# Moving GpSimd folds off a chunk's last slot, and packing the last transform stage one item to a slot

## The chip, the cores and the metric

One core of one Trainium2 chip. The metric is the device time of one execution in microseconds (us), the median of several executions. Engines are written as in the profile: PE is TensorE (matmuls), PEld its weight loads, ACT is ScalarE, DVE is VectorE, POOL is GpSimd, SP is SyncE, which here issues most DMAs. A "q" after an engine (SPq, ACTq) marks what its sequencer does, such as issuing a DMA.

## The reference, cut to what matters

```python
X = np.fft.fft(x, axis=1); X = np.fft.fft(X, axis=2)   # x: 8 x 3008 x 256, float32
x = X.real.reshape(24064, 256)
out = (gelu(x @ w_gate) * (x @ w_val)) @ w_out         # 256 -> 1536 -> 256
```

A real two-axis Fourier transform of each of 8 batches, then a gated feed-forward layer on every token.

## The kernel before

The order of the program is planned by hand. A batch's feed-forward work takes 36 slots: three chunks of columns (512, 512 and 481) by 12 blocks of the hidden dimension. Into these slots the plan puts the transform of the next batch: folds on POOL, stage 1 on PE, a trip through memory (Z), and nine last-stage items, three for each chunk: a row item (`tp_y`), an even item (`tp_e`) and an odd item (`tp_o`). I name a stretch of 36 slots after the batch that is *transformed* in it: stretch 3 transforms batch 3 while PE multiplies for batch 2.

```python
def tp_y(b, gi):                      # the row item: 4 x 128 numbers, copied by ACT, written to memory
    ...
    nc.scalar.activation(yr[:, :], ps[:4, 0:128], AF.Copy)
    nc.sync.dma_start(out=<yrow in memory, part gi>, in_=yr[:, :])

def tp_rows(b, gi):                   # one slot after the odd item of chunk gi
    nc.sync.dma_start(out=<EB, part gi, all 128 partitions>, in_=<yrow, part gi>)
    nc.sync.dma_start(out=<EO, odd half, part gi, 1 partition>, in_=<yrow, part gi>)   # "the odd row"

def plan():
    ...
    slot_of = [first + i * n // len(ops) for i in range(len(ops))]      # folds of batch b
    if b == 1: slot_of = [4, 4, 5, 5, ...]
    for s, f in zip(slot_of, ops): at(pool, s, f)
    if 1 < b < B - 1:                                                   # input loads for batch b + 1
        for k, piece in ((0, 1), (1, 3), (2, 4)):
            at(fill, slot_of[piece * per + 1] + 1, lambda b=b, k=k: load_part(b + 1, k))
    ...
    items = [tp_y(b, 0), tp_e(b, 0), tp_o(b, 0), tp_y(b, 1), ...]       # nine
    spread(b, items, s + 7, s0 + NS - 3)                                # from slot s + 7 to the stretch's slot 33
```

`load_part` with k = 0 is a pair of loads of 768 KB: the forward part by SP, the mirrored part by POOL. The writes to EO are tracked by tile: an odd item, which writes EO too, waits for the odd row's DMA of the chunk before it.

## Time and profile before

| | before |
|---|---|
| median of 3 executions | 630.39 us (629.39 to 630.58) |
| span of the profiled execution | 627.0 us |
| mean granted clock of PE | 0.996 |
| length of stretches 1 to 7, and of the last without transform | 78.17, 75.69, 74.04, 73.92, 73.92, 73.93, 72.91, 81.13 us |

The stretches are measured from the start of a first gate matmul to that of the next. Four of them last about 74 us, which is what PE's work takes. The prediction shows the busy times, the chain of waits and the waits.

It did not make the row quick: POOL's half of the pair had left at 224.96, the row took 4.7 us (by the semaphore updates it landed at 230.51, where such rows take 1.8 to 2.4 us in this trace with no load under way), and ACT waited half a microsecond for it:

```profile
230.59 0.60 ACT L592 ACTIVATE EO_sb<-ps_dft 128x512 bf16<-128x512 f32 x1 [0.51 <-DMA EO_sb<-yrow]
```

### The profile page before, as it was taken

The numbers are of one execution on the slowest core, as the hardware profiler recorded it, in microseconds if no ns is written. First come the engines' busy times: TensorE is split into PE (matmuls) and PEld (weight loads), VectorE is DVE, ScalarE is ACT, GpSimd is POOL, SyncE is SP. The second block draws the span as 40 slices with busy tenths as digits, with TensorE's granted clock in tenths as the row PEclk, the third lists the DMA queues.
The fourth block names the chain that finished last, engine by engine and source line by source line (L and its number), as shares of the span: only waits on it lengthen the run. The fifth ranks groups of instructions, "written<-read, shape, count | busy, mean of one in ns | idle before, by whom it ended". The sixth has DMA issues, their size and how long they took to land.

```text
span 627.0 us, 12895 instructions
## 1 busy us (share of the span) xinstructions
PE 612.3 (98%) x4195; PEld 405.1 (65%) x4243; DVE 578.3 (92%) x941; ACT 428.4 (68%) x842; POOL 505.3 (81%) x510
## 2 busy tenths in 40 slices
PE   7999999999999999999999999999999999999997
PEld 3456666666666666666666666666666666666666
DVE  8689989999899999999999998999999999999992
ACT  6777677666776677667676677676676666666661
POOL 8399999989897998879997899969988655555651
PEclk8999999999999999999999999999999999999999
DMA  9961754536353353731645335633212322221123
GB/s 177 227 97 31 210 129 116 144 105 159 99 146 101 98 133 79 184 113 46 160 110 135 101 78 127 148 97 98 62 49 63 91 86 55 51 52 39 42 51 81
DMA packets 54217, 65.40 MB, mean 104 GB/s; under 512 B 7831, under 2 KB 49802, under 8 KB 51754
## 3 DMA queue, kind: packets, MB, share of 16 engines
q1 hardware_dynamic: 47222, 49.03, 30.6%
q0 software_dynamic: 6608, 15.29, 11.4%
q8 instruction: 33, 0.54, 0.4%
q10 hardware_dynamic: 320, 0.26, 0.2%
q14 instruction: 34, 0.28, 0.2%
HBM read 39.65 MB, written 30.17 MB: 111 GB/s over the span
## 4 chain that ended last, share of the span: by engine, by line
PE 93%; ACT 2%; issue 1%; DVE 1%; DMA 1%; POOL 1%; POOLq 0%; ACTq 0%
PE ps_o L749 38%; PE ps_g L660 28%; PE ps_v L660 19%; PE ps_dft L546 2%; PE ps_dft L582 2%; PE ps_o L820 1%; DMA Z_sb<-z 1%; PE ps_dft L443 1%; PE ps_dft L612 0%; ACT gelu_sb L676 0%; POOL h_sb L724 0%; POOL eo_sb L224 0%; DMA out_dram<-out_sb 0%; ACT gelu_sb L685 0%; PE ps_dft L749 0%
## 5 line engine op out<-in xcount | busy, mean ns | idle before, releaser
L724 POOL TENSOR_TENSOR h_sb<-gelu_sb,v_sb 128x512 bf16<-128x512 bf16 (+1 forms) x280 | 319.8, 1146 | 93.1 <-DVE v_sb L722 85.9
L749 PE MATMUL ps_o<-Wo_sb,h_sb 128*128 128x256 bf16 (+1 forms) x2232 | 334.9, 273 | 0.9 <-POOL h_sb L724 0.9
L749 PEld LDWEIGHTS <-h_sb 128*128 128x128 bf16 (+1 forms) x2304 | 228.7, 100 | 112.9 <-POOL h_sb L724 2.6
L676 ACT ACTIVATE gelu_sb<-ps_g 128x512 bf16<-128x512 f32 (+1 forms) x288 | 169.4, 588 | 98.6 <-PE ps_g L660 80.9
L660 PE MATMUL ps_g<-EO_sb,W_sb 128*128 128x512 bf16 (+1 forms) x817 | 228.5, 375 | 3.8 <-ACT gelu_sb L685 0.8
L704 DVE SCALAR_TENSOR_TENSOR ve_sb<-EB_sb,yw,ps_v 128x512 f32<-128x512 bf16 (+1 forms) x280 | 206.3, 737 | 25.9 <-PE ps_v L660 25.0
L660 PE MATMUL ps_v<-EO_sb,W_sb 128*128 128x512 bf16 (+1 forms) x575 | 213.7, 375 | 0.7 <-DVE W_sb L451 0.6
L720 DVE TENSOR_TENSOR h_sb<-gelu_sb,ps_v 128x512 bf16<-128x512 bf16 (+1 forms) x280 | 189.9, 678 | 1.1 <-ACT gelu_sb L685 0.7
L660 PEld LDWEIGHTS <-W_sb 128*128 128x128 bf16 x1440 | 137.2, 98 | 81.1 <-issue 1.8
L722 DVE SCALAR_TENSOR_TENSOR v_sb<-ve_sb,ps_v 128x512 f32<-128x512 f32 (+1 forms) x280 | 187.5, 670 | 0.0
L685 ACT ACTIVATE gelu_sb<-ps_g 128x512 bf16<-128x512 f32 (+1 forms) x288 | 168.7, 586 | 0.0
L769 ACT ACTIVATE out_sb<-ps_o 128x512 f32<-128x512 f32 x92 | 55.0, 598 | 35.7 <-PE ps_o L749 35.6
L224 POOL TENSOR_TENSOR eo_sb<-ab_sb 94x512 bf16<-94x512 f32 (+1 forms) x70 | 77.6, 1111 | 0.5
L549 ACT ACTIVATE S_sb<-ps_dft 96x512 bf16<-96x512 f32 x56 | 32.9, 588 | 14.0 <-PE ps_dft L546 13.9
L592 ACT ACTIVATE EO_sb<-ps_dft 128x512 bf16<-128x512 f32 (+1 forms) x44 | 26.0, 590 | 23.3 <-PE ps_dft L582 22.1
L217 POOL TENSOR_TENSOR ab_sb<-x_raw,x_raw 94x508 f32<-94x508 f32 (+1 forms) x30 | 33.0, 1100 | 0.0
L220 POOL TENSOR_TENSOR ab_sb<-x_raw,x_raw 94x508 f32<-94x508 f32 (+1 forms) x30 | 32.9, 1098 | 0.0
L546 PE MATMUL ps_dft<-eo_sb,G 94*96 94x256 bf16 x119 | 22.5, 274 | 0.2 <-POOL eo_sb L224 0.2
L158 POOL DMA_INDIRECT x_raw<-in_x_dram,idx x18 | 17.1, 948 | 2.9 <-issue 1.1
L582 PE MATMUL ps_dft<-TP,Z_sb 128*128 128x128 bf16 (+1 forms) x184 | 17.8, 218 | 0.0
L582 PEld LDWEIGHTS <-Z_sb 128*128 128x128 bf16 x192 | 14.6, 98 | 1.8 <-DVE Z_sb L534 0.6
L546 PEld LDWEIGHTS <-G 94*96 94x96 bf16 x119 | 13.0, 123 | 1.2 <-issue 0.4
(148 smaller groups left out, 166.2 us busy)
## 6 DMA issues: line engine op xcount, KB each, us to landing
out_dram<-out_sb SPq DMA_DIRECT2D x364, 64.0 KB
x_raw<-in_x_dram SPq DMA_DIRECT2D x10, 768.0 KB
Z_sb<-z SPq DMA_DIRECT2D x7, 768.0 KB
z<-S_sb SPq DMA_DIRECT2D x7, 576.0 KB
EB_sb<-yrow SPq DMA_DIRECT2D x14, 128.0 KB
z<-S_sb SPq DMA_DIRECT2D x7, 192.0 KB
x_raw<-in_x_dram SPq DMA_DIRECT2D x2, 640.0 KB
EB_sb<-yrow SPq DMA_DIRECT2D x7, 120.2 KB
```

Of the source, the lines that this page charges most:

```text
L224: eng.tensor_tensor(_sub(eo, [[C, nj], [1, 128]], j0 * C + g * 128), ab(0, 0, [[1, 128]]), ab(1, 0, [[1, 128]]), op=op)
L546: nc.tensor.matmul(ps[:96, q * C : (q + 1) * C], G[:, j, :], _sub(eo, [[1, C]], j * C), start=(j == js[0]), stop=(j == js[-1]))
L582: nc.tensor.matmul(ps[:, o : o + n], st["Z"][:, pair, g * 128 : g * 128 + 128], _sub(TP, [[1, n]], g * 128), start=True, stop=True)
L660: nc.tensor.matmul(ps[:, :n], W[nm, part][:, fs], src, start=start, stop=stop, **kw)
L676: nc.scalar.activation(gl[:, 0, :n], pg[:, :n], AF.Gelu)
L685: nc.scalar.activation(_sub(gl, [[-1, n]], TOK + n - 1), pg[:, :n], AF.Gelu)
L704: nc.vector.scalar_tensor_tensor(ve[:, :n], EB_bufs[b][:, c0 : c0 + n], yw[:, fc : fc + 1], pv[:, :n], op0=ALU.mult, op1=ALU.add)
L720: nc.vector.tensor_tensor(st["h"][:, fc, 0, :n], gl[:, 0, :n], pv[:, :n], op=ALU.mult)
L722: nc.vector.scalar_tensor_tensor(_sub(vv, [[-1, n]], n - 1), ve[:, :n], 2.0, pv[:, :n], op0=ALU.mult, op1=ALU.subtract)
L724: nc.gpsimd.tensor_tensor(st["h"][:, fc, 1, :n], gl[:, 1, :n], vv[:, :n], op=ALU.mult)
L749: nc.tensor.matmul(pso[:m, half], st["h"][:, fc, sign, h0 : h0 + m], Wo_sb[:, fc, :], start=(fc == 0 and not (first and sign)), stop=(fc = ...
L769: nc.scalar.activation(_sub(osb, [[1, 2 * C]], 0, part_num=m), pso[:m, :], AF.Copy)
```

## The change

Its intent: POOL must not start a 1.2 us fold where the second layer at a chunk's end waits for POOL's multiply; and the last stage, one item a slot, should be finished before the stage 1 of the batch after begins, so that they don't meet on ACT. The core of the diff:

```diff
+            else:
+                slot_of = [s + {NFC - 1: 2, 0: 1}.get(s % NFC, 0) for s in slot_of]
...
-            spread(b, items, s + 7, s0 + NS - 3)
+            spread(b, items, s + 7, s0 + NS - 10 if b > 2 else s0 + NS - 3)
...
+    GATE2 = ()
```

The diff also adds code for a two-step gate (`e2_tile`, `make_ywg`, `l1_gate_odd`), all of it for the blocks named in `GATE2`. That is empty, so nothing of it is built; both programs have the same instructions on each engine, in another order.

More of the change, by code (lines that the diff above doesn't have):

```diff
@@ L135, in v_tile, with e2_tile @@
         return work([128, TOK], FP32, "v", 4, "v_sb")
+    def e2_tile():
+        return work([128, TOK], FP32, "e2", 1, "e2_sb")
     def osb_tile():
@@ L245 @@
     one_h = const_pool.tile([1, 1], BF16)
-    yw = const_pool.tile([128, NFC], FP32)
+    yw, ywg = (const_pool.tile([128, NFC], FP32, name=f"yw_{i}") for i in "vg")
     NGP = NJ * NK
@@ L477, in make_yw, with make_ywg @@
         return run
+    def make_ywg():
+        fcs = sorted({i % NFC for i in GATE2})
+        ps = psum("dft")
+        for fc in fcs:
+            nc.tensor.matmul(
+                ps[:, fc : fc + 1], W["g", "O"][0:1, fc * 128 : (fc + 1) * 128], one_h, start=True, stop=True)
+        for fc in fcs:
+            nc.scalar.activation(ywg[:, fc : fc + 1], ps[:, fc : fc + 1], AF.Copy, scale=2.0)
     EO_bufs, EB_bufs = {}, {}
@@ L634, in tp_o @@
         return tp_e(b, gi, 1, engine)
+    NS = NG * NFC
+    GATE2 = ()
     def store(b, gi, sub, sign, osb_half, queue):
@@ L667, in cols_of, with two_gate @@
             return n, c0, E, O, cstate[ci], slice(fc * 128, (fc + 1) * 128)
+        def two_gate(ci, fc):
+            return 0 < b < B - 1 and ci * NFC + fc in GATE2
         def l1_gate(ci, fc):
@@ L672, in run @@
                 pg = psum("g")
+                if two_gate(ci, fc):
+                    mm(pg, n, "g", "E", fs, E, True, True)
+                    e2 = e2_tile()
+                    nc.scalar.activation(e2[:, :n], pg[:, :n], AF.Copy, scale=2.0)
+                    st["ps"][fc] = [pg, gelu_tile(), e2]
+                    return
                 mm(pg, n, "g", "E", fs, E, True, False)
@@ L678, in l1_gate, with l1_gate_odd, run @@
             return run
+        def l1_gate_odd(ci, fc):
+            def run():
+                if not two_gate(ci, fc):
+                    return
+                n, c0, _, O, st, fs = cols_of(ci, fc)
+                pg, gl, e2 = st["ps"][fc][:3]
+                del st["ps"][fc][2]
+                mm(pg, n, "g", "O", fs, O, False, True, skip_group_check=True)
+                nc.scalar.activation(gl[:, 0, :n], pg[:, :n], AF.Gelu)
+                d = v_tile()
+                nc.vector.scalar_tensor_tensor(
+                    d[:, :n], EB_bufs[b][:, c0 : c0 + n], ywg[:, fc : fc + 1], pg[:, :n],
+                    op0=ALU.mult, op1=ALU.subtract)
+                nc.gpsimd.tensor_tensor(d[:, :n], e2[:, :n], d[:, :n], op=ALU.add)
+                st["ps"][fc][0] = d
+            return run
         def l1_gate2(ci, fc):
@@ L683, in run @@
                 pg, gl = st["ps"][fc][:2]
+                if two_gate(ci, fc):
+                    nc.scalar.activation(_sub(gl, [[-1, n]], TOK + n - 1), pg[:, :n], AF.Gelu)
+                    return
                 mm(pg, n, "g", "M", fs, O, False, True, skip_group_check=True)
@@ L777, in ffn_work @@
             parts = {k: [f(ci, fc) for fc in range(NFC)] for k, f in (
-                ("G", l1_gate), ("V", l1_value), ("g", l1_gate2), ("v", l1_value2))}
+                ("G", l1_gate), ("O", l1_gate_odd), ("V", l1_value), ("g", l1_gate2), ("v", l1_value2))}
             subs = [nsub - 1, *range(nsub - 1)] if last(ci) else range(nsub)
@@ L874, in behind_first_gate @@
         tp_y(0, 0)()
-    NS = NG * NFC
     def plan():
@@ L972, in feed @@
                 two.pop(0)()
+            parts["O"][fc]()
             for f in pool.pop(i, []):
```

## The prediction

> **What bounds the kernel now.** Per batch there are 36 slots (three chunks of 12); in each, PE does one block of the gate and value matmuls (5 of 512 or 481 columns) and two pieces of the second layer (8 of 256). Transform work of the next batches is put into slots: folds on POOL, stage 1 ("S") and the last stage on PE with a copy on ACT. I read first the page's busy times and chain.
>
> ```profile
> PE 612.3 (98%) x4195; PEld 405.1 (65%) x4243; DVE 578.3 (92%) x941; ACT 428.4 (68%) x842; POOL 505.3 (81%) x510
> PE 93%; ACT 2%; issue 1%; DVE 1%; DMA 1%; POOL 1%; POOLq 0%; ACTq 0%
> ```
>
> PE is the bound. A busy PE is not PE at its peak, so I took start-to-start times of its matmuls from the trace: 216 ns for 512 columns, 203 for 481, 109 for 256; a plain slot takes 5 x 216 + 8 x 109 = 1.95 us, and most slots of 172 to 600 us take exactly that plus what was put in. What PE loses after the first 25 us is therefore a short list of waits, which the waits view gives:
>
> ```profile
> PEld L749 <- POOL h_sb L724: 2.6, 6, 1.2
> PE ps_o L749 <- POOL h_sb L724: 0.9, 1, 0.9
> PE ps_g L660 <- ACT gelu_sb L685: 0.8, 2, 0.5
> ACT EO_sb L592 <- DMA EO_sb<-yrow: 1.1, 2, 0.6
> ```
>
> (engine, line, releaser: total us, times, longest.) The first two are what the change aims at. The last one, small now, decides my prediction. Its longest case, in the timelines of ACT and PE:
>
> ```profile
> 159.55 0.60 ACT L769 ACTIVATE out_sb<-ps_o 128x512 f32<-128x512 f32 x1 [0.37 <-PE ps_o L749]
> 160.76 0.60 ACT L592 ACTIVATE EO_sb<-ps_dft 128x512 bf16<-128x512 f32 x1 [0.61 <-DMA EO_sb<-yrow]
> ...
> 162.81 0.57 PE L660 MATMUL ps_g<-EO_sb,W_sb 128*128 128x481 bf16 x2 [0.46 <-ACT gelu_sb L685]
> ```
>
> ACT stood 0.61 us before the copy of an odd-part item, waiting for the one-row DMA of the item group before it; everything behind it on ACT was late, and PE's gate matmul, which needs a gate bank back from ACT two slots later, lost 0.62 us (start to start). This is batch 2, the only one whose last stage already runs one item a slot. The build confirms it as a rule: the odd item of group 1 (or 2) of every batch waits on a semaphore for the row DMA of group 0 (or 1).
>
> **The skill.** "DMA: Bandwidth & Descriptors", Queues, rings and completion order: on each DMA engine the descriptors of one issuer's queue are consumed in ring order. The trace agrees. The SP queue of batch 4's last stage:
>
> ```profile
> 299.65 0.33 SPq L152 DMA_DIRECT2D x_raw<-in_x_dram  x1
> 302.81 3.27 SPq L654 DMA_DIRECT2D out_dram<-out_sb  x4
> 306.18 0.93 SPq L626 DMA_DIRECT2D EB_sb<-yrow  x1
> 307.20 0.23 SPq L628 DMA_DIRECT2D EO_sb<-yrow  x1
> ```
>
> By the semaphore updates in the trace the 768 KB input load issued at 299.65 lands from 307.8 to 309.1; the stores issued at 302.81 land at 309.3 at the earliest, though such a store takes 1.9 us when no load is ahead of it. The same holds after each of the other loads I looked at. A row DMA with no load near takes 1.9 us.
>
> "TensorE: Matmul & The Clock Gate", Part 1: after an idle window of some 3.4 us the array runs at half clock until a busy window has passed. The opening shows it (last number but two: granted clock): PE busy 1.43 us of 3.41 was little enough to halve the next window.
>
> ```profile
> 7.78:11.19 3.41, 1.43 (x13) 0.81 (x14) 3.38 (x14) 3.33 (x11) 3.41 (x5) 1.00 1.09 200
> 11.19:14.61 3.41, 3.41 (x19) 1.74 (x18) 3.31 (x17) 2.59 (x6) 3.41 (x6) 0.50 1.27 168
> ```
>
> "Perfetto Trace Analysis", Tensor Engine Instruction: ACT, DVE and GPSIMD are strict FIFO, so work queued in front delays what is behind. The 0.62 us above and the fold below agree.
>
> **The change, part by part.** The set of two-step gates is empty, so all the new gate code is dead; the built programs have the same instructions on every engine, in another order. No work is added or removed.
>
> (a) Folds. From batch 2 on, folds in slot 11 of a chunk move two slots on, those in slot 0 move one. On POOL a fold (1.25 us) stands before the multiply that the second layer waits for. Worth: one stall of 1.06 us at 77 us (POOL finishes that multiply at 78.06, after a 1.25 us fold) and 86, 81 and 101 ns in batches 3 to 5, in all 1.33 us. But the 1.06 us is not gained: 1.5 slots later PE waits 0.35 us for the Z read, which landed at 80.5 and was issued at 76.22, before the stall; PE would only wait there instead. Left: 0.27 us.
>
> (b) Last stage, batches 3 to 7: its nine items end at slot 26 of the batch before instead of 33. The items cost PE the same wherever they stand (4 x 56 ns, or 0.25 us for a row item). ACT: an item at the end of a slot that also empties ps_o (every third) costs PE 126 to 138 ns if nothing follows in the next slot (slots at 112, 217, 261 us). The 138 ns in batch 3 goes; five odd items of group 2, and four stage 1 items that lose the row item beside them, now stand so: 9 x 0.13 - 0.14 - 0.3 (35 ns waits for ps_o that go) = +0.7 us.
>
> (c) The row DMA. Now the rows of a group are issued in slot j and the next odd item copied in slot j+2. In batches 3, 4 and 5 the big input load for a later batch sits between: the order on SP in the build is stores, input load, EB rows, EO row of group 1; and the odd item of group 2 waits for that EO row, which can't land before the load. (In the kernel before, the odd item came six slots after.) In batch 2 the moved fold takes the load with it, one slot later: it now stands before the rows of group 0 and after the stores.
> Batch 4, on the times of before: stores of slot 23 shift by one extra item, to 296.85, so they end about 299.25 and the load goes out at 299.4. The mirrored half, issued by POOL, goes out 1.1 us sooner as no fold is in front. Both end some 0.6 us sooner than before, 307.2 to 308.5, the row DMA 0.3 to 0.7 later: 307.5 to 309.2. PE has finished the odd item by 302.9 (slot 26 began at 300.10; three more items by its end, 0.22 + 0.25 + 0.21, plus 1.89 and 0.21), ACT would copy it at 303.1. Wait 4.4 to 6.1, say 5.3.
> Batch 3 in the same way (load out at 225.5 and landing 233.7 to 236.4, item ready at 229.1): 4.9 to 8.1, say 6.5. Batch 5 (load at 373.3, landing to 383.3, item at 377.0): 5.5. Batch 2: load out at 156.4 instead of 151.0, landing about 164 to 165, row at 163.9 to 165.5 where it was 160.7: 4.0 more than the 0.6 it has. Batches 6 and 7 have no load in this place: no wait.
> ACT is stopped and PE follows within two slots, so these waits fall on PE nearly whole: 5.3 + 6.5 + 5.5 + 4.0 = 21.3 us.
>
> (d) Clock. A PE stop of 4 to 6.5 us leaves at least one window emptier than the one above. Half clock then lasts, beyond the stop, 2.3 to 4 us depending on phase, of which half is lost: 1.5 us each, 4 times: 6 us (estimate from the window of 3.41 us in the trace).
>
> Sum: 630.4 - 0.3 + 0.7 + 21.3 + 6 = 658. I shade to 656, since the waits may overlap with something I count twice.
>
> **Rivals.**
> 1. The intent holds: POOL's waits go, the ACT collisions of stage 1 and last stage thin out, and the row DMA isn't late. 629 to 631. For it: the stalls named are real, and a tuned kernel's author expects it. Against: their whole worth is 0.3 us, and the 0.61 us wait in batch 2 shows the dense order already touching the row DMA without a load straight in front.
> 2. The rows wait for the load, but less: the row's ring is done with its share of the load early, and the clock doesn't drop. Then 4 x 3.5 us: 644. For it: the 16 parts of a load land over 1.3 to 2.5 us. Against: the earliest part is already 4 us after the item.
> 3. The dense items alone make ACT the bound in these eight slots: 2 gate copies, an item and a third of an emptying, 3.3 x 0.49 us = 1.6 us, against 2.1 us of PE: no.
>
> **Range and chances.** With every wait at its low end and no clock loss: 630.4 + 4.4 + 4.9 + 4 + 3.1 + 0.4 = 647; at the high end with 2 us of clock each: 630.4 + 25.9 + 8 = 664. I take 643 to 666. Two per cent slower is 643.0. Slower needs some 13 us of the 27; I give 0.90. Same, 0.09: the row DMA gets past the load. Faster would need 12.6 us that PE hasn't got to give: 0.01.
>
> **What would show it.** ACT's wait for EO_sb<-yrow grows from 1.1 us to 20 or more, in four events of 4 to 8 us at about 160, 229, 309 and 390 us; PE waits for gelu_sb as long, the granted clock falls to half right after each, and batches 6 and 7 take as long as before (74 us). The 1.06 us wait on POOL is gone and the wait for Z_sb is 1.4 us. Wrong: if those four are under 1 us, (c) is wrong and the time is 630; if they are there without half clock, (d) is wrong and it is 650.

## More of the kernel before

The page's row of granted clock, one digit for each 40th of the span (9 is 90% or more):

```profile
PEclk8999999999999999999999999999999999999999
```

Only the opening has a slice below full clock. And SP's timeline in stretch 3 (start, length of the issue, line, destination<-source):

```profile
225.83 0.24 SPq L628 DMA_DIRECT2D EO_sb<-yrow  x1
226.22 0.27 SPq L152 DMA_DIRECT2D x_raw<-in_x_dram  x1
226.58 0.38 SPq L618 DMA_DIRECT2D yrow<-yrow_sb  x1
```

Here the odd row leaves just ahead of SP's 768 KB load (L152).

## The result, and the profile after

| | before | after |
|---|---|---|
| median | 630.3 us (629.39 to 630.58, 4 runs) | 657.25 us (653.85 to 659.96, 4 runs) |
| profiled span, granted clock | 627.0 us, 0.996 | 653.8 us, 0.984 |
| opening | 19.08 | 18.04 |
| stretch 1 | 78.17 | 79.40 |
| stretch 2 | 75.69 | 78.61 |
| stretch 3 | 74.04 | 81.83 |
| stretch 4 | 73.92 | 81.42 |
| stretch 5 | 73.92 | 82.06 |
| stretches 6, 7, last | 73.93, 72.91, 81.13 | 74.03, 73.05, 81.13 |

The ratio is 1.0427 (95% interval 1.0372 to 1.0483): slower. Ratios here and below are the mean time of one kernel's fast runs over the mean of the other's in the same rounds, so not quite the ratio of the medians.

The loss sits in stretches 2 to 5. The page of the changed kernel (busy times, granted clock, chain):

```profile
PE 619.8 (95%) x4195; PEld 408.3 (62%) x4243; DVE 578.8 (89%) x941; ACT 429.7 (66%) x842; POOL 505.9 (77%) x510
...
PEclk9999999999899989999799997999999999999999
...
PE 81%; DMA 9%; POOL 4%; ACT 2%; issue 2%; DVE 1%; POOLq 0%; SPq 0%; ACTq 0%
```

PE's instruction count is the same and its busy time grew by 7.5 us, about the half-clock loss found below; four slices have a lower clock. DMA's share of the chain went from 1% to 9%. The waits, as engine, line, releaser: total us, times, longest:

```profile
ACT EO_sb L605 <- DMA EO_sb<-yrow: 17.7, 4, 5.7
PE ps_g L677 <- ACT gelu_sb L731: 16.9, 5, 5.8
```

The first was 1.1 us in two events before. PE's wait for ACT follows it with nearly the same total. One event in full, in stretch 3. SP's timeline:

```profile
229.49 0.53 SPq L155 DMA_DIRECT2D x_raw<-in_x_dram  x1
230.12 1.61 SPq L639 DMA_DIRECT2D EB_sb<-yrow  x1
231.82 0.25 SPq L641 DMA_DIRECT2D EO_sb<-yrow  x1
```

Load, EB rows, odd row: the order is turned round. By the semaphore updates in the trace the 16 parts of the load land from 237.92 to 238.97 and the row at 238.39. ACT's timeline (in brackets: idle before, and what ended it) and PE's:

```profile
232.78 0.60 ACT L815 ACTIVATE out_sb<-ps_o 128x512 f32<-128x512 f32 x1 [0.39 <-PE ps_o L795]
238.47 0.57 ACT L605 ACTIVATE EO_sb<-ps_dft 128x481 bf16<-128x481 f32 x1 [5.10 <-DMA EO_sb<-yrow]
```

```profile
234.24 0.60 PE L795 MATMUL ps_o<-Wo_sb,h_sb 128*128 128x256 bf16 x4
240.02 1.21 PE L677 MATMUL ps_g<-EO_sb,W_sb 128*128 128x481 bf16 x3 [5.18 <-ACT gelu_sb L731]
```

ACT stands before the copy of the odd item until the row has landed (238.39, copy at 238.47); the gate copies behind it are late, and PE gets its gate bank back 5.18 us late. What comes then is in the windows (length, then busy time and instructions of PE, PEld, DVE, ACT, POOL, granted clock, DMA share, GB/s):

```profile
234.50:240.20 5.70, 0.52 (x5) 0.25 (x3) 1.24 (x3) 1.50 (x3) 2.80 (x5) 1.00 0.76 182
240.20:243.62 3.42, 3.42 (x14) 1.93 (x13) 1.33 (x3) 1.03 (x2) 2.17 (x2) 0.50 0.19 36
```

After the stop, 3.42 us at half clock. Such windows follow the stops of all four stretches: 165.11, 240.20, 318.71 and 400.63, of 3.41, 3.41, 6.83 and 6.83 us. In the last two PE also stood still for part of the window, so that it lost 1.67, 1.67, 2.30 and 2.18 us start to start, not half of the window.

Two smaller stops. The first is the input of the last stage in stretch 1, the second stage 1 in stretch 3 behind a fold on POOL:

```profile
80.70 0.22 PE L625 MATMUL ps_dft<-TP,Z_sb 128*4 128x128 bf16 x1 [2.13 <-DMA Z_sb<-z]
...
188.81 0.38 PE L559 MATMUL ps_dft<-eo_sb,G 94*96 94x256 bf16 x2 [0.67 <-POOL eo_sb L227]
```

The wait at 78 us for POOL's multiply (1.06 us) is gone, and PE waits for Z instead, 2.29 us start to start: Z landed at 80.65, where it had landed at 80.46. The wait behind the fold, 0.84 us start to start, is new. The shift moved two folds of batch 3 into one slot; it also moved POOL's input load (issued at 186.52, 0.94 us on POOL) right in front of the fold that PE waits for. No run separates the two.

Where the 26.8 us of the two profiled spans went, by start-to-start times of PE:

| term | us |
|---|---|
| waits for the odd row, stretches 3, 4, 5: 5.34, 5.22, 5.97 | 16.5 |
| the same in stretch 2: 2.10 - 0.62 | 1.5 |
| half clock after them: 1.67 + 1.67 + 2.30 + 2.18 | 7.8 |
| wait for the fold in stretch 3 | 0.8 |
| stretch 1: 2.29 for Z in place of 1.06 + 0.35 | 0.9 |
| opening, 1.04 shorter in this execution | -1.0 |
| sum (the rest, 0.3, is many small ones) | 26.5 |

### The profile page after: what moved, and what is told of

Its sections match the earlier page's. It is cut to its first block, busy times and chain, and to the rows that moved or that the text cites. A ratio compares the mean times of both kernels' runs of the same rounds, so it can differ in the third digit from the quotient of the medians.

```text
span 653.8 us, 12885 instructions
## 1 busy us (share of the span) xinstructions
PE 619.8 (95%) x4195; PEld 408.3 (62%) x4243; DVE 578.8 (89%) x941; ACT 429.7 (66%) x842; POOL 505.9 (77%) x510
## 4 chain that ended last, share of the span: by engine, by line
PE 81%; DMA 9%; POOL 4%; ACT 2%; issue 2%; DVE 1%; POOLq 0%; SPq 0%; ACTq 0%
PE ps_o L795 34%; PE ps_g L677 26%; PE ps_v L677 17%; DMA EO_sb<-yrow 3%; DMA w_raw<-in_moe_w_gate_dram 2%; PE ps_dft L559 2%; DMA Wo_sb<-in_moe_w_out_dram 2%; POOL h_sb L770 2%; PE ps_dft L595 1%; DVE v_sb L768 1%; ACT gelu_sb L702 1%; DMA yrow<-yrow_sb 1%; POOL eo_sb L227 1%; DMA Z_sb<-z 1%; POOL w_raw L426 1%
## 5 line engine op out<-in xcount | busy, mean ns | idle before, releaser
L750 DVE SCALAR_TENSOR_TENSOR ve_sb<-EB_sb,yw_v,ps_v 128x512 f32<-128x512 bf16 (+1 forms) x280 | 206.2, 737 | 50.5 <-PE ps_v L677 48.1
L677 PE MATMUL ps_g<-EO_sb,W_sb 128*128 128x512 bf16 (+1 forms) x817 | 231.1, 379 | 20.0 <-ACT gelu_sb L731 16.9
L815 ACT ACTIVATE out_sb<-ps_o 128x512 f32<-128x512 f32 x92 | 55.0, 598 | 34.6 <-PE ps_o L795 34.5
```

The source lines that it names most:

```text
L677: nc.tensor.matmul(ps[:, :n], W[nm, part][:, fs], src, start=start, stop=stop, **kw)
L750: nc.vector.scalar_tensor_tensor(ve[:, :n], EB_bufs[b][:, c0 : c0 + n], yw[:, fc : fc + 1], pv[:, :n], op0=ALU.mult, op1=ALU.add)
L815: nc.scalar.activation(_sub(osb, [[1, 2 * C]], 0, part_num=m), pso[:m, :], AF.Copy)
```

## The experiments

Theory at the start: in stretches 3 to 5 the 768 KB load is issued ahead of the odd row, the odd item two slots later waits for that row, and PE then loses more at half clock. Rivals: the folds on POOL, the dense items on ACT, or the load's traffic itself are to blame. Twelve kernels ran, all correct, in three calls; "before" was timed beside each (medians 630.13, 629.96 and 630.05 us).

| run | median us (range, runs) | ratio to before, 95% |
|---|---|---|
| folds_only | 631.86 (631.18 to 635.29, 5) | 1.0025 [1.0008, 1.0042] |
| stage_only | 653.62 (652.84 to 657.13, 6) | 1.0372 [1.0355, 1.0390] |
| load_later | 631.29 (631.05 to 631.75, 4) | 1.0021 [1.0005, 1.0038] |
| row_late | 632.30 (631.17 to 633.25, 4) | 1.0040 [1.0024, 1.0057] |
| row_other_queue | 647.49 (644.52 to 648.84, 4) | 1.0263 [1.0226, 1.0299] |
| warm | 650.21 (648.37 to 652.60, 4) | 1.0310 [1.0273, 1.0348] |
| best | 630.75 (630.19 to 632.73, 6) | 1.0012 [0.9988, 1.0037] |
| best2 | 630.41 (629.50 to 632.81, 6) | 1.0004 [0.9978, 1.0030] |
| rows_act_queue | 630.00 (628.75 to 630.97, 4) | 0.9999 [0.9976, 1.0023] |
| half_load | 647.10 (645.70 to 649.47, 4) | 1.0263 [1.0239, 1.0286] |
| mirror_later | 642.23 (640.75 to 643.96, 4) | 1.0198 [1.0171, 1.0225] |
| best3 | 630.38 (627.86 to 630.84, 6) | 0.9995 [0.9974, 1.0016] |

### Each part of the change alone: folds_only, stage_only

```diff
  folds_only (from after)
-            spread(b, items, s + 7, s0 + NS - 10 if b > 2 else s0 + NS - 3)
+            spread(b, items, s + 7, s0 + NS - 3)
  stage_only (from after)
-                slot_of = [s + {NFC - 1: 2, 0: 1}.get(s % NFC, 0) for s in slot_of]
+                slot_of = list(slot_of)
```

> The changed kernel with the last stage spread as before; only the folds are moved. My theory (the row DMA lands behind the input load): no load stands between rows and odd items in batches 3 to 5, so only batch 2 waits (about 2.1 us of PE instead of 0.6, because the load moved with the fold), then one half-clock window (1.7 us), and 0.84 us for POOL's late fold at the second stage 1 of batch 3; minus 0.27 us: 630.3 + 1.5 + 1.7 + 0.8 - 0.3 = 634. Rival (the folds moved onto other slots are what costs, by POOL's backlog): 645 or more.

> The changed kernel with the folds where they were; only the last stage is dense. My theory: the three waits of 5.2 to 6.0 us stay (16.5 us) with their half-clock time (6 us), batch 2 is as before: 630.3 + 16.5 + 6 + 0.3 = 653. Rival (the folds are the cause): 630 to 633.

The folds alone cost 0.25% (631.86 us), the last stage alone 3.7% (653.62 us): nearly all of the loss is the last stage. ACT's wait for the odd row in folds_only, then in stage_only:

```profile
ACT EO_sb L605 <- DMA EO_sb<-yrow: 3.2, 2, 2.2
```

```profile
ACT EO_sb L605 <- DMA EO_sb<-yrow: 17.3, 3, 5.9
```

In folds_only the stop of stretch 2 is there (2.39 us start to start) and those of stretches 3 to 5 are not; in stage_only it is the other way round, with stops of 5.79, 6.19 and 6.06 us. So the fold shift makes the stop in stretch 2 and the last stage the other three. folds_only also has the wait for a fold in stretch 3 (0.83 us); stage_only hasn't. The 634 us expected for folds_only counted half clock after the stop of stretch 2; none followed the stop there.

### Taking away the order of load and row: load_later, row_late

```diff
  load_later (from after; batches b = 3 to 6)
-                    at(fill, slot_of[piece * per + 1] + 1, lambda b=b, k=k: load_part(b + 1, k))
+                    late = {3: 71, 4: 100, 5: 136, 6: 172}.get(b) if k == 0 else None     # behind the last rows
+                    at(fill, late or slot_of[piece * per + 1] + 1, lambda b=b, k=k: load_part(b + 1, k))
  row_late (from after): the odd row goes once for each batch, after its last chunk
+            if gi < NG - 1: return
-            nc.sync.dma_start(out=<EO, odd half, part gi>, in_=<yrow, part gi>)
+            nc.sync.dma_start(out=<EO, odd half, all parts>, in_=<yrow, all parts>)
```

> The changed kernel with the first part of each input load (batches 4 to 7) issued after the last row DMA of the stage beside it instead of before the rows; nothing else moved. My theory: ACT's wait for the row falls from 17.7 us to under 1.5, the clock stays full, time 630.3 + 0.8 (POOL's fold) + 1 (ACT collisions) = 632. Rival A (nine dense items are too much for ACT or POOL whatever the DMA does): 645 or more. Rival B (the load hurts wherever it is, by sharing the DMA engines): part of the waits stays, 638 to 648.

> The changed kernel with its loads where they are, but the odd part's row written once a batch, by one DMA after the third group, so that no odd item has a row DMA in front of it. My theory: no wait for the row at all although each load still precedes it on the queue: 630 to 632, and the 0.6 us that batch 2 loses even in the kernel before goes too. Rival (the load itself slows ACT or PE, not the wait on the row): still 645 or more.

Both keep the folds and the dense items of the changed kernel, and give back all but 0.2% and 0.4%. In neither trace does ACT wait for EO_sb<-yrow at all, and the clock of load_later is full throughout:

```profile
PEclk9999999999999999999999999999999999999999
```

So neither the dense items nor the shifted folds make the time; the pair of load and row does. row_late keeps the load where it is, so the load's traffic alone costs nothing either. It has a price of its own: in stretch 2 PE waits 1.39 us for the one late row.

### Does the row wait because of its queue? row_other_queue, rows_act_queue

```diff
  row_other_queue (from after)
-            nc.sync.dma_start(out=<EO, odd half, part gi>, in_=<yrow, part gi>)
+            nc.scalar.dma_start(out=<EO, odd half, part gi>, in_=<yrow, part gi>)
  rows_act_queue: the same, and in tp_y
-            nc.sync.dma_start(out=<yrow in memory, part gi>, in_=yr[:, :])
+            nc.scalar.dma_start(out=<yrow in memory, part gi>, in_=yr[:, :])
```

> The kernel after, with the odd row's DMA issued by ScalarE instead of SyncE, so that it stands in another issuer's queue than the 768 KB load. My theory (the row waits behind the load because both go through the same issuer's queue, in order): the row lands about 2 us after its issue, the odd item no longer waits, and the time falls to about 632 us, as where the load is moved away. Rival (the load fills the 16 shared DMA engines, so that a row from any queue waits): the waits stay and the time stays at 650 to 657 us. In between, 638 to 648: both take part.

It came out between the two theories, at 647.49 us, and for a reason that neither had named. Its waits, and the timelines of SP and ACT in stretch 3:

```profile
ACT gelu_sb L702 <- DMA yrow<-yrow_sb: 14.2, 3, 5.3
```

```profile
227.43 0.52 SPq L155 DMA_DIRECT2D x_raw<-in_x_dram  x1
...
229.68 0.33 SPq L631 DMA_DIRECT2D yrow<-yrow_sb  x1
```

```profile
237.63 0.21 ACTq L641 DMA_DIRECT2D EO_sb<-yrow  x1
237.95 0.58 ACT L702 ACTIVATE gelu_sb<-ps_g 128x481 bf16<-128x481 f32 x1 [5.26 <-DMA yrow<-yrow_sb]
```

The odd row that the odd item needs went out ahead of the load and cost nothing. But ACT must issue the next one in its own order of work, and could not before that row had been written to memory (its last part landed at 237.56); that write was still on SP, behind the load. ACT stood there, with its gate copies behind. The wait had moved from a copy to a DMA issue.

> The kernel after, with both small transfers of a row on ScalarE's queue: the write of the row to memory and the odd row's read of it. In the run before this one only the read was moved, and ScalarE then stood still for the write, which was still behind the 768 KB load in SyncE's queue. My theory (what counts is the order within the queue of one issuer): write and read now take 1 to 2 us each even while the load is under way, no odd item waits, and the time is about 632 us. Rival (the load and its mirror fill the shared DMA engines, whatever the queue): write and read take 5 us and more while the load is under way, ScalarE stands still for them, and the time stays at 645 us or above.

With the write moved as well the time is that of before, 630.0 us. ACT's issues in stretch 3, then SP's load:

```profile
223.51 0.22 ACTq L641 DMA_DIRECT2D EO_sb<-yrow  x1
...
224.98 0.25 ACTq L631 DMA_DIRECT2D yrow<-yrow_sb  x1
...
229.88 0.22 ACTq L641 DMA_DIRECT2D EO_sb<-yrow  x1
```

```profile
225.51 0.53 SPq L155 DMA_DIRECT2D x_raw<-in_x_dram  x1
```

The time is as my theory expected, but the landings do not bear its reason out. The row and the write that somebody waits for left *before* the load, and landed 1.4 and 1.3 us after their issue. (POOL's half of the pair left at 225.07, also after them.) The row of 229.88, issued 4.4 us after the load on the other queue, landed at 235.74: 5.9 us, 0.2 us after the load's last part (235.51). In the three other stretches with a load it is the same: 4.9, 4.7 and 5.2 us where a row of this trace with no load under way takes 1.4 to 1.7. Nobody waits for that last row so soon, which is why it costs nothing. A queue of its own did not let a row past a load; what helped was to be on the way before either half of the pair: against ACT's emptying copy of that slot (L815, at 232.78 in after, 228.78 here) ACT issued the row 5.3 us ahead and SP only 1.0 us. The half of my theory about "the order within the queue of one issuer" is not shown, and the rival's half, that a row from any queue waits while the load runs, is what these four landings say. In stretch 2 the row of ACT's queue (160.40 to 165.29) was late although SP's load had landed at 162.19, with POOL's under way until 166.00.

### What is it that the row waits for? half_load, mirror_later

```diff
  half_load (from after; batches b = 3 to 6, k == 0)
+  at the load's old place:  load_forward(b + 1, 13, 4)   # 384 KB, SP
+                            load_mirror(b + 1, 9, 8)     # 768 KB, POOL, unchanged
+  behind the last rows:     load_forward(b + 1, 9, 4)    # the other 384 KB
  mirror_later
+  at the load's old place:  load_forward(b + 1, 9, 8)
+  behind the last rows:     load_mirror(b + 1, 9, 8)
```

> The kernel after, with the load cut in two: 384 KB go where the 768 KB went, and the other 384 KB behind the last rows, in batches 3 to 6. If the wait is the time that the bytes ahead of the row take, the waits of 5.3, 5.2 and 6.0 us shrink by about the half of the 5.6 us that such a load takes when it is alone, to about 2.5 to 3 us each, the half clock by a part, and the time is about 645 us. Rival A (any load ahead of the row costs a fixed latency): 655 us. Rival B (the other load, of the mirror by GpSimd, is what takes the time): 652 to 657 us.

> The kernel after, with the mirror's load on GpSimd's queue (768 KB as well) put behind the last rows in batches 3 to 6, and SyncE's load left where it is. If the two loads share the engines, the load ahead of the row lands after about 5.6 us, as it did in batch 2 where the mirror went out later, instead of 8 to 9.5 us: the three waits shrink by about 3 us each and the time is about 645 us. Rival (the row waits for its own queue alone, and the mirror costs it nothing): 655 us.

ACT's waits for the row in half_load (three events) and in mirror_later (of its four events one is that of stretch 2):

```profile
ACT EO_sb L605 <- DMA EO_sb<-yrow: 11.3, 3, 4.2
```

```profile
ACT EO_sb L605 <- DMA EO_sb<-yrow: 8.5, 4, 2.4
```

| stretch 3 | load issued (SP) | row issued (SP) | load landed | row landed | stops of PE in stretches 3, 4, 5 |
|---|---|---|---|---|---|
| after | 229.49 | 231.82 | 237.92 to 238.97 | 238.39 | 5.34, 5.22, 5.97 (mean 5.51) |
| half_load | 227.08 | 229.06 | 233.89 to 234.83 | 234.98 | 4.34, 3.26, 4.44 (mean 4.01) |
| mirror_later | 229.21 | 231.48 | 233.96 to 235.10 | 235.03 | 2.27, 2.20, 2.66 (mean 2.38) |

Half of SP's load takes 1.5 us off a stop, about half of the 2.8 that I expected (647.1 us against 645). The whole of POOL's load takes 3.1 us off, as expected; the time, 642.2 us, is below the 645, as only one of its three stops was followed by half clock. So more than half of the stop comes from a load that stands in *another* queue than the row. How it does so this run leaves open: the row landed with SP's load here too (235.03 and 235.10), so POOL's load may have delayed the row itself, or SP's load that the row stands behind. For the first speak the row of the kernel before that left ahead of SP's load and behind POOL's (4.7 us), and the row in stretch 2 of rows_act_queue.

### Is the half clock a cost of its own? warm

```diff
+            if i in (100, 136, 172):           # ahead of the gate that stops in stretches 3, 4 and 5
+                ps = psum("dft")
+                for _ in range(22):
+                    nc.tensor.matmul(ps[:, :], W_sb[:, 0, 0:128], W_sb[:, 0, 0:512], start=True, stop=True)
```

> The kernel after, with 22 extra 512-column matmuls of constant data into a spare accumulator bank just ahead of the gate of slots 100, 136 and 172, which is where TensorE stands still for 5.2 to 6.0 us in batches 3, 4 and 5. They take about 22 x 0.22 = 4.8 us, less than each stop, and nobody reads the result. My theory (after a stop TensorE runs at half clock for 3.4 or 6.8 us, which lost 1.67 + 2.30 + 2.18 = 6.15 us in these three batches of the trace): the granted clock stays at full there, the waits themselves stay, and the time falls to about 651 us. Rival (the half clock costs nothing beside the wait): the time stays at 657 us, or grows if the extra work does not fit inside the stops.

650.21 us. PE's timeline in stretch 3 (one of the 22 records is missing) and the clock of the execution:

```profile
236.06 4.70 PE L1015 MATMUL ps_dft<-W_sb 128*128 128x512 bf16 x21
242.08 0.77 PE L677 MATMUL ps_g<-EO_sb,W_sb 128*128 128x481 bf16 x3 [1.32 <-ACT gelu_sb L731]
```

```profile
PEclk9899999999999999999999999999999999999999
```

The wait is still there: 22 x 0.216 = 4.75 us of idle matmuls and 1.49 us of standing still make 6.2 us. But the clock stays full after the opening, and the time falls by 7.0 us where I expected 6.15. The surplus has a candidate in the trace: this execution had no half clock in stretch 2 either, though nothing was done there. Useless matmuls of course don't beat the kernel before; they show what the clock cost.

### Versions that were to beat both: best, best2, best3

```diff
  best (from before): the odd row as in row_late; b == 2: fold slots 23 and 24 -> 25; b > 3: fold slot s0 -> s0 + 1;
-                spread(b, items, s + 6, s + 18)                 # batch 1
+                spread(b, items, s + 8, s + 18)
  best2: best, and in stage 1
+                    if b > 1 and g == 0 and jg < 2 and s % 3 == 1: s += 1
  best3 (from before): only b == 2's fold slots and batch 1's items
```

> From the kernel before: the odd row goes by one DMA for each batch after its last group; two folds on GpSimd in front of batch 2's stage 1 go one slot later, and so do those in the first slot of later batches' chunks; batch 1's items start two slots later. Removed small stops as read from the trace of before: 1.1 us for a fold and 0.35 us for an input at batch 2, 0.3 us and 0.6 us at the items of batches 1 and 2, so I expect 628 us against 630.3. Rival (these stops are hidden behind other waits, which take their place): 630.3 us, within 0.2%.

> As best, and the pairs of stage 1 tiles start a slot later where their second one would fall into the slots in which TensorE also has a row item. By my theory this takes away another 0.5 to 1 us of short waits: 627.3 us. Rival: nothing more than best, or a new wait at the end of a batch, 628 to 630 us.

> The kernel before, with two small shifts alone: the two folds in front of batch 2's stage 1 one slot later, and batch 1's items two slots later; the odd rows stay as they were (in the runs best and best2 the one late row for each batch made batch 2's first gate wait 1.4 to 1.9 us). Stops of before that these take away: 1.06 us for the fold, 0.35 us for the input, some 0.3 us in batch 1. I expect 629 us against 630, which 5 rounds may just tell from the same. Rival: the input of batch 1's last stage comes no sooner, so the stop turns up there again, and the time is the same.

All three are the same as before within their intervals. The expected 0.1 to 0.5% did not come. In best and best2 the single late row made PE wait in stretch 2 (1.43 and 1.94 us). best3's trace has stretch 1 at 76.53 us instead of 78.17, so the stops for the fold and for Z are gone; but its opening took 20.61 us instead of 19.08, and a wait of 0.8 us for a row, shown here, is new at the first gate of the next batch:

```profile
98.15 0.58 PE L660 MATMUL ps_g<-EO_sb,W_sb 128*128 128x512 bf16 x2 [0.64 <-DMA EO_sb<-yrow]
```

The opening varies from execution to execution (18.04 to 21.32 us over all the traces), so one trace can't tell how much of it belongs to the kernel; the timed runs say that nothing was won.

## Why the prediction was right

**The result** was 657.25 us against 656 predicted, well inside the range. By its own steps:

**(b), (c) The waits for the row: right in mechanism, mis-sized in one term.** Stretches 3, 4 and 5 were put at 6.5, 5.3 and 5.5 us and measured 5.3, 5.2 and 6.0. Stretch 2 was put at 4.0 more and measured 1.5: I had the row land at 163.9 to 165.5, and it landed at 162.12. I took for that load the 8 us of the other ones; it took 5.6, because here POOL's mirrored load left only after it (157.42 against 156.46). mirror_later shows the same in the other stretches: without the mirrored load, 5.9 to 6.1 us. The trace of before had it already: SP's load of stretch 2 took 5.7 us there (151.00 to 156.67), with POOL's issued at 153.31. Sum predicted 21.3, measured 18.0. load_later and row_late confirm the pair of load and row as the cause; folds_only confirms that in stretch 2 it is the fold shift that takes the load along. One remark of (c) is off: in the kernel before, the odd item came five slots after the slot of the row (four for the first row of stretch 3), not six.

**The reason given for the row's lateness was too narrow.** That the row "can't land before the load" held (it landed among the load's last parts), but I rested it on what the Trainium skill says of one issuer's ring order ("DMA: Bandwidth & Descriptors", Queues, rings and completion order). Rows issued by ACT while the pair of loads was under way were late as well. The same page's section "Issuing engines are not separate DMA queues" says that DMAs of all issuers run on the same 16 engines; the 4.7 to 5.9 us of those rows agree with it, and this is the sentence that I should have built on. Whether ring order adds anything to it, no run here separates.

**(d) The clock: right, a little small.** 6 us predicted, 7.8 measured in the trace; warm took 7.0 off the time by keeping PE busy. Three of the four half clocks are as argued. The one in stretch 2 is partly luck: it was forecast for a stop of 4.6 us and came after one of 2.10 (three waits close together), while stops of 2.2 to 2.4 us in folds_only, warm and mirror_later, in the same stretch, were not followed by it.

**(a) The folds: one wait missed.** That the gain at 78 us would be repaid at the Z read was right in kind, at 2.29 us instead of 1.4, in an execution whose opening was 1.04 us shorter while Z landed at nearly the same time. Not foreseen was the 0.84 us behind a fold in stretch 3, where the shift puts two folds of batch 3 into one slot and an input load of POOL in front of one (0.83 in folds_only, none in stage_only).

**The small ACT collisions** of the last stage with stage 1 were put at +0.7; the table leaves 0.3 for all small terms, so they are of that size at most.

The overshoot of the waits (3.3 us) and the misses (1.8 of clock, 0.8 of fold) nearly cancel, and I had shaded the sum of 658 to 656. So the closeness of 656 to 657.25 is partly luck; the sign and the order of size are not.

**The rivals.** The intent's gain (629 to 631) is refuted by folds_only and stage_only: each part alone is slower. load_later keeps both parts without the late row, and gains nothing either (631.29). The second rival (smaller waits, no loss of clock, 644) is what mirror_later looks like, 642.2 us, but not this kernel. ACT as the bound is refuted by load_later and row_late, which have the same dense items.

## What to carry to other kernels

When you move work earlier in a hand-made order, ask of every small DMA which large one now leaves ahead of it, and who waits for the small one two slots later; here a 1 KB row that came late in four batches cost 18 us, through a copy on ACT that stood in front of PE's gate banks. A queue of its own does not protect a small transfer from a large one under way, and neither does leaving just ahead of one half of a pair: send it before any of them leaves, or give its reader slack. And a stop of an engine that is the bound can cost more than its length, here another 1.7 to 2.3 us of half clock for each.

## What the Trainium skill lacked or had wrong

- "DMA: Bandwidth & Descriptors", Queues, rings and completion order, says that each DMA engine takes turns between queues by packets, which reads as if a small transfer in another queue would soon be served. It gives no figure for it. Here a 1 KB row on ScalarE's queue took 4.7 to 5.9 us from issue to landing while large loads (up to 768 KB each) were under way in the queues of SyncE and GpSimd, and 1.4 to 1.7 us otherwise. No page has a figure either for what a load in another queue can add to such a wait: 3.1 of 5.5 us here.
- "TensorE: Matmul & The Clock Gate", Part 1, speaks of an idle window of some 3.4 us. In these traces stops of 2.86 us and more were followed by half clock every time (12 of 12), and of eight between 2.1 and 2.7 us two were as well. A stop shorter than the window can be enough, and not always is.
- No page has a figure for issuing a DMA right behind a large one: SP's issue of the 128 KB rows took 1.20 to 1.64 us behind its load (stretch 3 of eight traces), and in after 0.51 us for the same size one chunk earlier, with no load in front.
